# VectorE order, early loads of partial sums, and two row blocks per chunk in a fused convolution and token-mixing kernel

## The chip, the cores and the metric

The kernel runs on one core of one Trainium2 chip. The metric is device time in microseconds (us) of one execution, given as the median of several. Shorter is better. Each execution comes with the TensorE clock that was granted to the core.

The names of the engines are those of the profile: PE is TensorE (matmuls), PEld its weight loads, DVE is VectorE, ACT is ScalarE, POOL is GpSimd and SP is SyncE. An L with a number is a line of the kernel in question, so the same operation has other line numbers in other kernels.

## The reference

The inputs are x of 8 x 4224 x 192 (batch, tokens, channels), seven convolution taps for each of 8 heads, a 192 x 192 matrix for theta, two 4224 x 4224 token-mixing matrices and a 192 x 192 channel matrix. Cut to what matters:

```python
# causal 7-tap convolution over tokens, one softmaxed filter per head
x = conv(x, softmax(weight))
theta = x @ w_theta
zr = x * np.cos(theta)
zi = x * np.sin(theta)
y = np.einsum('ts,bsd->btd', w_tok_r, zr) + np.einsum('ts,bsd->btd', w_tok_i, zi)
u = x + y
return u + np.maximum(u @ w_ch, 0.0)
```

The token mixing is nearly all of the arithmetic: for each of 33 row blocks of 128 output tokens it sums over 33 chunks of 128 input tokens, for 8 x 192 = 1536 columns.

## The kernel before

The kernel makes three passes. In each it builds 11 chunks (convolution, theta, sines, products, all kept on chip), and for each of the 33 row blocks it adds those 11 chunks' share of the mixing to a partial sum in DRAM. A row block has three pieces of 512 columns, and a piece of one pass is 22 matmuls of 512 columns, so a row block of one pass has 66. The chunks of passes 2 and 3 are built in small steps between the mixing of the pass before. Only the first pass has nothing to hide its chunks behind, so its first row block is mixed chunk by chunk, in the order in which the chunks appear. In the last pass the partial sum is loaded, the convolved x is added (the residual), the mixing is added, the channel matrix is applied and the result is stored.

One chunk is a chain over three engines (cuts are marked):

```python
def build_chunk(p, c, xws, zs):
    for hp in range(H // 4):
        pc = mmps.tile([P, 2, PC], F32, name="pc", tag="mm")
        ...                                   # 8 convolution matmuls
        for k in range(2):
            nc.scalar.activation(out=xz[...], in_=pc[...], func=AT.Copy)   # L180
        yield
    ...                                       # store of xz to DRAM (xs)
    for g in range(NG):
        xTs.append(transposed(xf[:, g * GC : (g + 1) * GC]))   # 6 transposes, VectorE copy
        yield
    for g in range(NG):
        channel_mix(th, xTs[g], wth)          # 8 matmuls of 192 columns
        nc.vector.tensor_scalar(out=ang...)   # clamp
        nc.scalar.activation(out=zr[...], func=AT.Sin, ...)
        nc.scalar.activation(out=zi[...], func=AT.Sin)
        ...                                   # zr *= x, zi *= x on VectorE
        yield
```

The first row block takes three accumulators, `ys`, and mixes each chunk into all three as it appears:

```python
def chunk_major(tb, p, wts):
    ys = [yps.tile([P, PC], F32, name="y", tag="y") for _ in range(NP)]     # NP = 3
    for c in range(PASSES[p]):
        for j in range(NP):
            next(first, 0); next(first, 0)    # two steps of the chunks being built
            mix(ys[j], wts, zs[p], c, j, PASSES[p])
```

All other row blocks go through this loop. `begin_rows` loads the sums of the next row block and adds the residual, `finish_piece` evicts a finished piece:

```python
def begin_rows(tb, p):
    pv = wk.tile([P, N], F32, name="pv", tag="pv", bufs=3)
    if p:
        nc.sync.dma_start(out=pv, in_=part[p - 1][tb, :, :])
    if p == len(PASSES) - 1:
        nc.sync.dma_start(out=xr, in_=xs[rows, :])
        for j in range(NP):                                                   # L295
            nc.vector.tensor_tensor(out=pv[:, cols], in0=pv[:, cols], in1=xr[:, cols], op=ALU.add)

def finish_piece(tb, j, y, p, pv, ub):
    ...
        nc.vector.tensor_tensor(out=pv[:, cols], in0=y, in1=pv[:, cols], op=ALU.add)   # L305
    ...
        nc.scalar.activation(out=ub[:, cols], in_=pv[:, cols], func=AT.Copy)           # L310

for j in range(NP):
    for c in range(ncs):
        mix(y, wts, zs[p], c, j, ncs)
        ...            # steps of the next pass's chunks, of the output of the block before
    finish_piece(tb, j, y, p, pv, ub)
    if j == 0 and tb + 1 < NT:
        pv_next = begin_rows(tb + 1, p)
```

The order of the instructions on TensorE is pinned: each TensorE instruction gets an order dependence on the one before it, without a semaphore. On the other engines a scheduler in the framework chooses the order.

## Time and profile before

| what | before |
|---|---|
| median of 3 runs | 1776.66 us (1775.98 to 1779.78) |
| span of the profiled run | 1780.6 us, granted clock 0.970 |
| store of the first row block, pass 1 | issued at 131.4 us |
| store of the third row block, pass 1 | issued at 166.2 us |
| from there to the last store of pass 1 | 463.0 us |
| pass 2, between its last store and that of pass 1 | 513.6 us |
| last store of pass 2 to the last eviction | 630.1 us |
| period of a row block, pass 3 | 19.04 us |

The parts of the table come from the times at which SyncE issued the stores; a period is the mean distance between the first output stores of successive row blocks. In the middle of the kernel a row block is a floor: 66 matmuls at 0.2155 us are 14.2 us, and TensorE does nothing else but build the next pass's chunks. So the two ends matter.

First, the page's busy shares, and two of its rows of 40 slices (each digit is a tenth of a slice of 44.5 us; PEclk is the granted clock in tenths):

```profile
PE 1667.8 (94%) x8910; PEld 767.8 (43%) x8910; DVE 857.3 (48%) x1471; ACT 229.3 (13%) x366; POOL 517.5 (29%) x948
PE   4889999999999999999999999898888998888898
PEclk9559999999999999999999999999999999999999
```

94% looks like a kernel with 6% to gain. The Trainium skill (Perfetto Trace Analysis, section "Identifying the Most-Contended Engine") warns that the matmuls' busy share is not a good measure of how close TensorE is to its peak, because matmuls are pipelined. The slices show one reason why that holds here: in slices 2 and 3 the clock was at half, and a slow matmul counts as busy. (The 9 of the first slice is no measurement: the page takes the clock as full until the first record, and that comes at 30.7 us.) From slice 26 on, in the last pass, it falls to 8 or 9 tenths.

The windows view of before has, for each stretch, its length, then the busy time of PE, PEld, DVE, ACT and POOL with their instruction counts, the granted clock, the DMA share and GB/s. The first stretch lies in the stage in which pass 1's chunks are built, the second in the last pass:

```profile
45.00:70.00 25.00, 21.05 (x125) 9.79 (x125) 12.75 (x22) 13.08 (x23) 10.47 (x18) 0.50 0.80 111
1600.00:1700.00 100.00, 87.97 (x488) 40.72 (x486) 50.33 (x91) 9.45 (x15) 21.54 (x40) 1.00 0.61 139
```

In the stage a chunk took 10.1 us (the first transposes of successive chunks are that far apart), with the clock at 0.50 from 37.5 to 133.1 us; matmuls of 512 columns start 0.40 to 0.43 us apart there, and 0.2155 in the middle of the kernel. The waits view of before tells what the last pass waits for (engine, line, waited for: us in total, times, longest us):

```profile
DVE pv L295 <- DMA pv<-part_84: 177.2, 33, 8.6
...
PE tp L223 <- ACT ub L310: 42.9, 29, 5.8
...
PE v L235 <- DVE uT L225: 28.4, 28, 1.0
```

VectorE waits in each of the 33 row blocks, for the partial sums; that would cost nothing if nobody needed VectorE. But TensorE waits for `ub` and `uT`, which come from behind VectorE. The timeline of VectorE (start, duration, line, operation, and in brackets the idle time before it with what ended it) shows one block:

```profile
1601.51 0.56 DVE L225 COPY uT<-tp 128x768 bf16<-128x768 bf16 x1 [2.67 <-PE tp L223]
1607.04 0.69 DVE L295 TENSOR_TENSOR pv<-pv,xr 128x512 f32<-128x512 f32 x1 [4.97 <-DMA pv<-part_84]
1607.65 0.68 DVE L305 TENSOR_TENSOR pv<-y,pv 128x512 f32<-128x512 f32 x1
```

The residual addition (L295) is for the next row block. VectorE stood idle for 4.97 us before it because the sums were not there, and the eviction of the current block's finished piece (L305) stood behind it. The chain of waits shows the loop that follows (start, us, what):

```profile
1596.69 6.03 DMA out_dram<-pv
...
1602.77 4.09 DMA pv<-part_84
...
1607.04 0.10 DVE pv L295
...
1607.65 0.03 DVE pv L305
...
1614.81 0.94 DVE pv L323 x2
...
1615.77 6.09 DMA out_dram<-pv
```

The output transfer of one block (6.03 us) frees a buffer, the sums of a later block are loaded into it (4.09 us), the residual takes them, the eviction behind it follows, and from it the next output. One round is 19.1 us, and the matmuls fit into it with room to spare.

### The profile page before, as it was taken

Reading aid. Unit: us, or ns where it says so; the run is one execution under the profiler, and the core shown is the slowest. Engines: PE = TensorE matmul, PEld = TensorE weight load, DVE = VectorE, ACT = ScalarE, POOL = GpSimd, SP = SyncE. Lnnn points to the kernel's source line nnn. Section 1 sums busy time; section 2 is a strip of 40 time slices with the busy share of each in tenths; the row PEclk is TensorE's granted clock in tenths of the full one; section 3 lists DMA queues with packets and bytes.
Section 4 is the critical chain, followed back from the end, with each engine's and each line's share of the span. In section 5 each row is a group of like instructions: output and inputs, shape, how many; then the busy total and the mean of one; then the engine's idle time right before and its main releaser. Section 6 shows DMA issues by size and latency. Waiting matters only on the chain.

```text
span 1780.6 us, 22353 instructions
## 1 busy us (share of the span) xinstructions
PE 1667.8 (94%) x8910; PEld 767.8 (43%) x8910; DVE 857.3 (48%) x1471; ACT 229.3 (13%) x366; POOL 517.5 (29%) x948
## 2 busy tenths in 40 slices
PE   4889999999999999999999999898888998888898
PEld 2334444444444444444444444344444443344344
DVE  6554444444444444444444444455445445544554
ACT  3541111111111001011111111001000000000010
POOL 6414333333333233323333322222112112211210
PEclk9559999999999999999999999999999999999999
DMA  9867666666666687777887766756556655665562
GB/s 132 114 101 130 121 117 121 128 118 112 125 121 118 127 186 163 171 163 173 177 178 170 164 157 159 173 124 149 134 139 138 146 133 129 140 146 139 126 144 70
DMA packets 232807, 248.31 MB, mean 139 GB/s; under 512 B 72192, under 2 KB 207360, under 8 KB 232704
## 3 DMA queue, kind: packets, MB, share of 16 engines
q0 software_dynamic: 167616, 91.14, 41.6%
q1 hardware_dynamic: 65088, 155.77, 24.7%
q8 instruction: 69, 1.13, 0.3%
q14 instruction: 34, 0.28, 0.0%
HBM read 247.07 MB, written 90.83 MB: 190 GB/s over the span
## 4 chain that ended last, share of the span: by engine, by line
PE 59%; DMA 18%; DVE 13%; issue 2%; DVEq 0%; ACT 0%; SPq 0%
PE y L278 54%; DMA out_dram<-pv 10%; DMA pv<-part_84 8%; DVE pv L323 3%; DVE pv L295 2%; PE pc L172 1%; PE th L235 1%; DVE pv L305 1%; PE tp L223 1%; PE th L240 1%; DVE uT L225 1%; DMA part_84<-pv 1%; PE v L235 0%; PE v L240 0%; DVEq L268 0%
## 5 line engine op out<-in xcount | busy, mean ns | idle before, releaser
L259 POOL DMA_DIRECT2D st<-in_moe_w_tok_i_dram x396 | 213.8, 549 | 1036.6 <-DVE wt_10979 L268 15.9
L259 POOL DMA_DIRECT2D st<-in_moe_w_tok_r_dram x396 | 214.6, 555 | 22.5 <-issue 4.2
L305 DVE TENSOR_TENSOR pv<-y,pv 128x512 f32<-128x512 f32 x198 | 134.8, 681 | 156.9 <-PE y L278 156.8
L225 DVE COPY uT<-tp 128x768 bf16<-128x768 bf16 x132 | 72.7, 551 | 169.8 <-PE tp L223 169.5
L295 DVE TENSOR_TENSOR pv<-pv,xr 128x512 f32<-128x512 f32 x99 | 67.0, 680 | 177.2 <-DMA pv<-part_84 177.2
L209 ACT ACTIVATE zr<-ang,half_pi 128x768 bf16<-128x768 f32 x66 | 61.6, 933 | 671.0 <-DVE ang L204 671.0
L310 ACT ACTIVATE ub<-pv 128x512 bf16<-128x512 f32 x99 | 62.4, 630 | 600.8 <-DVE pv L305 600.8
L303 DVE COPY pv<-y 128x512 f32<-128x512 f32 x99 | 67.2, 678 | 109.8 <-PE y L278 109.7
L204 DVE TENSOR_SCALAR ang<-th 128x768 f32<-128x768 f32 x66 | 62.8, 952 | 96.4 <-PE th L240 96.1
L180 ACT ACTIVATE xz<-pc 128x384 bf16<-128x384 f32 x132 | 56.1, 486 | 264.9 <-PE pc L172 142.8
L223 PE MATMUL tp<-ident,ub 128*128 128x128 bf16 x396 | 38.0, 220 | 42.9 <-ACT ub L310 42.9
L235 PEld LDWEIGHTS <-uT 128*128 128x128 bf16 x528 | 39.2, 101 | 82.3 <-DVE uT L225 41.8
L235 PE MATMUL v<-wch,uT 128*128 128x192 bf16 x264 | 44.4, 250 | 28.4 <-DVE uT L225 28.4
L323 DVE SCALAR_TENSOR_TENSOR pv<-v,pv 128x384 f32<-128x384 f32 x132 | 66.0, 539 | 7.3 <-PE v L240 7.3
L223 PE MATMUL tp<-ident,xz 128*128 128x128 bf16 x396 | 41.8, 248 | 15.0 <-DVE uT L225 7.1
L223 PEld LDWEIGHTS <-ub 128*128 128x128 bf16 x396 | 27.7, 98 | 63.3 <-ACT ub L310 47.9
L212 ACT ACTIVATE zi<-ang 128x768 bf16<-128x768 f32 x66 | 54.6, 828 | 0.0
L235 PE MATMUL th<-wth,uT 128*128 128x192 bf16 x264 | 51.0, 281 | 0.0
L214 DVE TENSOR_TENSOR zr<-xz,zr 128x768 bf16<-128x768 bf16 x66 | 36.3, 550 | 29.2 <-ACT zr L209 29.2
L223 PEld LDWEIGHTS <-xz 128*128 128x128 bf16 x396 | 31.6, 111 | 37.7 <-ACT xz L180 18.4
L240 PEld LDWEIGHTS <-uT 64*128 64x128 bf16 x528 | 25.7, 94 | 47.4 <-issue 47.4
L172 PEld LDWEIGHTS <-bands 96*64 96x64 bf16 x528 | 25.8, 127 | 43.8 <-issue 25.4
(759 smaller groups left out, 3780.6 us busy)
## 6 DMA issues: line engine op xcount, KB each, us to landing
st<-in_moe_w_tok_r_dram POOLq DMA_DIRECT2D x396, 88.0 KB, 5.4
st<-in_moe_w_tok_i_dram POOLq DMA_DIRECT2D x396, 88.0 KB, 3.6
part_83<-pv SPq DMA_DIRECT2D x33, 768.0 KB, 3.3
pv<-part_83 SPq DMA_DIRECT2D x33, 768.0 KB, 7.5
part_84<-pv SPq DMA_DIRECT2D x33, 768.0 KB, 3.3
pv<-part_84 SPq DMA_DIRECT2D x33, 768.0 KB, 4.2
out_dram<-pv SPq DMA_DIRECT2D x66, 384.0 KB, 5.0
xs<-xz SPq DMA_DIRECT2D x132, 96.0 KB, 4.5
```

The costliest lines, as they stand in the source:

```text
L204: nc.vector.tensor_scalar(out=by_bank(ang[:, :, :]), in0=banks(th), scalar1=-CLAMP, scalar2=CLAMP, op0=ALU.max, op1=ALU.min,)
L209: nc.scalar.activation(out=zr[:, cols], in_=af, func=AT.Sin, bias=half_pi[:], scale=1.0)
L223: pe(nc.tensor.transpose(tp[:, k, :], u[:, k * P : (k + 1) * P], ident))
L225: nc.vector.tensor_copy(out=uT[:], in_=tp[:])
L235: pe(nc.tensor.matmul(v[k], lhsT=tT[:, 3 * q + 2 * k, :], rhs=w[:, 2 * k, :], start=True, stop=False,))
L259: nc.gpsimd.dma_start(out=st[a * Q : (a + 1) * Q, :, 0 : ncs * Q], in_=w[tb * P : (tb + 1) * P, t0 : t0 + ncs * Q].rearrange("(bt i) s -> ...
L278: pe(nc.tensor.matmul(y, lhsT=wts[m][:, c, :, :].rearrange("p bt i -> p (bt i)"), rhs=zs[c][m][:, cols], start=(c == 0 and m == 0), stop=( ...
L295: nc.vector.tensor_tensor(out=pv[:, cols], in0=pv[:, cols], in1=xr[:, cols], op=ALU.add)
L303: nc.vector.tensor_copy(out=pv[:, cols], in_=y)
L305: nc.vector.tensor_tensor(out=pv[:, cols], in0=y, in1=pv[:, cols], op=ALU.add)
L310: nc.scalar.activation(out=ub[:, cols], in_=pv[:, cols], func=AT.Copy)
L323: nc.vector.scalar_tensor_tensor(out=pk, in0=banks(v)[:, k, :, :], scalar=0.0, in1=pk, op0=ALU.max, op1=ALU.add,)
```

## The change

The change has five parts that matter here (the diff also loads the mixing weights earlier and places their transposes). They are meant to remove the in-order stall of the last pass and to fill TensorE in the stage of the first chunks.

1. From the second row block on, VectorE's order is pinned to program order, as TensorE's was. The residual is placed one piece at a time, just before the end of a piece of the row block before.
2. The sums of row block q+2 are asked for at the start of the last piece of row block q.
3. In the first stage every chunk is mixed into five accumulators: three pieces of the first row block and two of the second. All temporary results share three banks, and the chunk's steps are interleaved with the mixing.
4. The convolution's bands are built in two halves, so that the first matmul can start earlier.
5. The 16 token rows in front of a chunk (the halo) are copied on chip from the chunk before, not loaded again.

The diff, cut to its core:

```diff
-    def pe(ins): ...
+    def in_order(engine, ins):
+        if engine in last:
+            tc.add_manual_dep(ins.ins, last[engine].ins.name, NOSYNC, reason="order")
+        last[engine] = ins
+        return ins
+    pinned = [False]
+    def dve(ins):
+        return in_order("dve", ins) if pinned[0] else ins
 ...
-    for k in range(KS):
-        nc.vector.tensor_tensor(out=bview or btmp, ...)
+    for hs in (slice(0, H // 2), slice(H // 2, H)):
+        for k in range(KS):
+            nc.vector.tensor_tensor(out=bview[:, hs] if k == 0 else btmp[:, hs], ...)
 ...
+                if before is not None:
+                    nc.sync.dma_start(out=hist, in_=before.xw[lo + Q : lo + Q + HALO, h, :, :])
 ...
-    def chunk_major(tb, p, wts): ...          # three accumulators
+        open_psum(stack, 5, 3)
+        y0 = [bank("y", "y") for _ in range(NP)]
+        y1 = [bank("y", "y") for _ in range(2)]
+        def mixes(i):
+            for ys, q, c in ((y0, 0, i - 2), (y1, 1, i - 3)):
+                for j, y in enumerate(ys):
+                    if 0 <= c < nc0:
+                        mix(y, weights[q], zs[0], c, j)
+                        yield
+        for i in range(nc0 + 3):
+            ...
+            for half in range(2):
+                if old:
+                    old.theta(half)
+                next(m, 0)
+                if ch:
+                    ch.conv(2 * half)
+                    ch.conv(2 * half + 1)
+                if old:
+                    old.times_x()
+                next(m, 0)
+            ...
+        begin_rows(1)
+        begin_rows(2)
+        for j in range(2):
+            sums[1].add(j, y1[j])
+    pinned[0] = True
 ...
-                if j == 0 and tb + 1 < NT:
-                    pv_next = begin_rows(tb + 1, p)
+                if q + 1 < len(seq) and c == ncs - 2 and sums[q + 1].final:
+                    sums[q + 1].residual(j)
+                if j == NP - 1 and c == 0:
+                    begin_rows(q + 2)
```

## The prediction

> **What bounds the kernel now.** The page gives TensorE 94% busy over 1780.6 us, but the stages differ. In the timeline the 512-column mixing matmuls start 0.2155 us apart at full clock; a row block of one pass has 66, so 14.2 us. From the first and last mixing matmul of each block:
> - Start: first matmul at 13.5 us, when VectorE has finished `bands` (waits view).
> - First row block, built chunk by chunk, until 130 us. The windows view shows TensorE 84-87% busy at granted clock 0.50 from 45 to 110 us; a chunk takes 10.1 us. The chain is serial (convolution, ScalarE copy, transpose, VectorE copy, theta), with gaps of 0.7 to 1 us. The Trainium skill (TensorE: Matmul & The Clock Gate, Part 1) says the clock is halved until TensorE has been busy for a whole window of about 3.4 us; this trace agrees in that 0.50 ends at 133 us, when mixing becomes dense.
> - Rest of passes 1 and 2: 130 to 1138 us, TensorE 100% busy. 65 blocks of 14.2 plus 22 chunks at about 3.75 make 1007 us: at its floor.
> - Last pass: 1138 to 1772 us, 19.2 us a block against about 16.7 (14.2, plus twice 0.35 of transposes and 0.9 of channel mix, from the timeline). The waits view has TensorE waiting 42.9 us for `ub` and 28.4 for `uT`. The chain of waits is a loop of one block: output transfer 6.1 us, load of the partial sums into the freed buffer 4.2, then 8.8 of VectorE work in order. The scheduler put the residual addition ahead of the eviction of the current row block, so VectorE sits 5 us (177 in all) on a load while TensorE needs it.
> - Tail: 8.7 us.
>
> **What the change does.**
> 1. Pinned VectorE order, load issued a block earlier: output, sums and `xr` land about 20 to 22 us after the start of the block in which they are freed, and the residual asks for them at about 21 (estimate from 6.1, 4.2 and 6.0 us). Small VectorE waits remain, no TensorE wait. Last pass about 553 us instead of 634.
> 2. First pass: mixing for five accumulators stands between the dependent steps. Per chunk at full clock TensorE has about 5.2 us, ScalarE 5.1, VectorE 5.3, so I expect 6 to 6.5 us a chunk after a DMA-bound start (weights of three blocks, 6 us of all queues each, compete with x). At halved clock TensorE would be busy without gaps, which should release it. The stage, now with two thirds of block 2, ends at about 103 us; before, that point is about 142.
> 3. Half-size bands first: start 2 to 3 us earlier (included).
> 4. Halo on chip: a third fewer x packets (1536 to 1024 a chunk, 56 ns, 16 queues: -1.8 us of DMA); it helps only the first stage.
>
> Sum: 103 + 487 (rest of pass 1) + 510 + 553 + 9 = 1662, less 4 for the difference between profile and timing: about 1660 us, 8 in 10 between 1638 and 1692.
>
> **What would show it.** Last pass: blocks of 16.7 us, TensorE's waits for `ub` and `uT` nearly gone. First stage: granted clock near 1.0 from about 40 us, 6 to 6.5 us a chunk. Middle unchanged at 15.4 us a block.
>
> **What would make it wrong.** The clock stays at 0.50 in the first stage (+25 to 30 us); three banks for all temporary results make the chunk loop serial again; the freed buffer still comes late and the loop of output, load, residual binds (+20 to 40); in-order halo copies on the sync queue hold up sums and stores.
>
> Chances: faster by over 2% 0.96, within 2% 0.03, slower 0.01.

## The result, and the profile after

The changed kernel took 1673.88 us in the median of 4 runs (1672.72 to 1675.82), with a right result; before took 1777.4 in the same rounds. The ratio is 0.9417, with a 95% interval from 0.9401 to 0.9434. A ratio here is the mean time of one kernel's fast runs over the mean of the other's fast runs of the same rounds, so it is not quite the ratio of the medians that I quote.

| part of the profiled span, us | before | after | difference |
|---|---|---|---|
| start to the store of the third row block of pass 1 | 166.2 | 139.6 | -26.6 |
| rest of pass 1 | 463.0 | 463.0 | 0.0 |
| pass 2 | 513.6 | 510.0 | -3.6 |
| last store of pass 2 to the last eviction | 630.1 | 550.7 | -79.4 |
| the rest (tail) | 7.7 | 7.7 | 0.0 |
| span | 1780.6 | 1671.0 | -109.6 |

So nearly three quarters of the gain came from the last pass and a quarter from the first stage. The rest of pass 1 did not move. Pass 2 lost 3.6 us; it takes 510.0 in before_edge (below) too, so the order on VectorE alone gives these. A row block of the last pass took 16.73 us instead of 19.04.

The same lines of the page after:

```profile
PE 1618.1 (97%) x8738; PEld 759.3 (45%) x8910; DVE 870.9 (52%) x1550; ACT 231.0 (14%) x366; POOL 509.7 (31%) x948
PE   4889999999999999999999999999999999999998
PEclk9999999999999999999999999999999999999999
```

TensorE's row no longer falls towards the end, and no slice has a clock of 0.5. (172 matmul records are missing from this trace: 8738 against 8910 weight loads.) The windows view after, at about the same places:

```profile
45.00:70.00 25.00, 21.99 (x173) 10.48 (x175) 16.49 (x33) 14.57 (x24) 11.70 (x21) 0.89 0.94 148
1500.00:1600.00 100.00, 99.21 (x551) 47.36 (x559) 61.82 (x108) 11.33 (x18) 25.74 (x48) 1.00 0.68 161
```

In the first stretch TensorE was hardly busier than before (21.99 us against 21.05) and did 173 matmuls where it had done 125: the clock was 0.89 against 0.50. In the last pass its busy share went from 88% to 99%.

In the waits view after, the wait for the partial sums is gone, and of TensorE's waits for `ub` and `uT` in the last pass 0.4 and 0.7 us are left. Two of the lines that are left for VectorE and TensorE:

```profile
DVE pv L364 <- PE y L331: 249.3, 154, 3.5
...
PE th L276 <- ACT xz L209: 10.5, 6, 3.1
```

VectorE waits for TensorE, as it should where TensorE is the bottleneck. The second line is new, and the experiments come back to it. The timeline of VectorE in the last pass after:

```profile
1594.35 0.68 DVE L354 TENSOR_TENSOR pv<-pv,xr 128x512 f32<-128x512 f32 x1
1595.60 0.69 DVE L364 TENSOR_TENSOR pv<-y,pv 128x512 f32<-128x512 f32 x1 [0.57 <-PE y L331]
```

The residual (L354) starts without any idle time in front of it, and the eviction (L364) waits for nothing but its matmuls. The page puts the chain that ended last, by engine, as follows, before and then after:

```profile
PE 59%; DMA 18%; DVE 13%; issue 2%; DVEq 0%; ACT 0%; SPq 0%
```

```profile
PE 93%; issue 1%; ACT 1%; DVE 1%; DMA 1%; SPq 0%; DVEq 0%; ACTq 0%
```

### The profile page after: what moved, and what is told of

It is laid out like the page before. It is cut to its first block, busy times and chain, and to the rows that moved or that the text cites. A ratio compares the mean times of both kernels' runs of the same rounds, so it can differ in the third digit from the quotient of the medians.

```text
span 1671.0 us, 22525 instructions
## 1 busy us (share of the span) xinstructions
PE 1618.1 (97%) x8738; PEld 759.3 (45%) x8910; DVE 870.9 (52%) x1550; ACT 231.0 (14%) x366; POOL 509.7 (31%) x948
## 3 DMA queue, kind: packets, MB, share of 16 engines
q0 software_dynamic: 152256, 85.24, 41.7%
## 4 chain that ended last, share of the span: by engine, by line
PE 93%; issue 1%; ACT 1%; DVE 1%; DMA 1%; SPq 0%; DVEq 0%; ACTq 0%
PE y L331 84%; PE tp L260 2%; PE v L276 2%; PE v L281 1%; PE th L276 1%; PE pc L202 1%; PE th L281 1%; DMA xs<-xz 1%; ACT xz L209 0%; ACT zi L245 0%; DVE ang L237 0%; DVE uT L264 0%; SPq L220 0%; DVE zi L251 0%; DVE pv L362 0%
## 5 line engine op out<-in xcount | busy, mean ns | idle before, releaser
L364 DVE TENSOR_TENSOR pv<-y,pv 128x512 f32<-128x512 f32 x198 | 136.6, 690 | 258.6 <-PE y L331 249.3
L237 DVE TENSOR_SCALAR ang<-th 128x384 f32<-128x384 f32 x132 | 67.5, 551 | 78.9 <-PE th L281 78.9
L209 ACT ACTIVATE xz<-pc 128x384 bf16<-128x384 f32 x132 | 57.7, 487 | 285.0 <-PE pc L202 169.2
L187 POOL DMA_DIRECT2D xw<-in_x_dram x132 | 76.7, 592 | 66.4 <-PE pc L202 55.3
L354 DVE TENSOR_TENSOR pv<-pv,xr 128x512 f32<-128x512 f32 x99 | 66.3, 670 | 0.0
L276 PE MATMUL th<-wth,uT 128*128 128x192 bf16 x264 | 47.2, 259 | 10.7 <-ACT xz L209 10.5
L202 PE MATMUL pc<-xw,bands 96*64 96x192 bf16 x528 | 38.5, 264 | 15.2 <-DMA xw<-in_x_dram 12.2
L202 PEld LDWEIGHTS <-bands 96*64 96x64 bf16 x528 | 22.2, 113 | 44.5 <-issue 31.4
L260 PE MATMUL tp<-ident,xz 128*128 128x128 bf16 x396 | 37.5, 233 | 2.1 <-ACT xz L209 1.8
```

Of the source, the lines that this page charges most:

```text
L187: nc.gpsimd.dma_start(out=self.xw[lo : lo + n, h, :, :], in_=x[:, t0 : t0 + n, :].rearrange("b s d -> s b d"),)
L202: pe(nc.tensor.matmul(pc[half * 2 * Q : (half + 1) * 2 * Q, hh * B * G : (hh + 1) * B * G], lhsT=bands[:, h, :, :].rearrange("p a m -> p ( ...
L237: dve(nc.vector.tensor_scalar(out=every_other(ang[:, :, :], k), in0=pair(th[k]), scalar1=-CLAMP, scalar2=CLAMP, op0=ALU.max, op1=ALU.min,))
L260: pe(nc.tensor.transpose(tp[:, k * P : (k + 1) * P], u[:, k * P : (k + 1) * P], ident))
L276: pe(nc.tensor.matmul(v[k], lhsT=tT[:, 3 * q + 2 * k, :], rhs=w[:, 2 * k, :], start=True, stop=False,))
L354: dve(nc.vector.tensor_tensor(out=self.pv[:, cols], in0=self.pv[:, cols], in1=self.xr[:, cols], op=ALU.add,))
```

## The experiments

Twelve kernels were run, and each gave a right result. The runs below went beside the kernel before. Each expectation was put before its run; where one names a theory by a letter, the text ahead of it says in words what was in question. For nopin, one_ahead, before_pin and one_block the trace that was kept is of another execution (spans of 1770.6, 1672.5, 1697.9 and 1690.3 us) than the views quoted (1767.2, 1673.9, 1696.1 and 1688.6); it shows the same waits, and figures taken from it are marked as kept.

### What gave the gain of the last pass

The prediction gave the last pass two causes in one breath: the pinned order of VectorE, and the load that is issued a block earlier. A third possibility was that neither is needed in full, and that one pair of instructions is the matter.

**nopin.** The changed kernel, with VectorE's order left to the scheduler.

```diff
-    pinned[0] = True
+    pinned[0] = False
```

> The changed kernel with VectorE's order left to the scheduler everywhere; the load two row blocks ahead and all else kept. Built, its VectorE order again has the residual addition of row block q+2 ahead of the last eviction of row block q. Theory A (the fixed order is what frees the last pass): that addition asks for its sums about 3 to 4 us before they land, TensorE waits for ub again, blocks of the last pass take 17.5 to 19.2 us instead of 16.75, time 1700 to 1755 us. Theory B (the earlier load is what frees it): blocks stay at 16.75, time 1670 to 1680.

It took 1768.29 us (1766.84 to 1771.91), a ratio of 0.9936 (0.9921 to 0.995). The gain is nearly gone, more so than theory A had it (1755 us at most); a block of the last pass takes 19.56 us in the kept trace. The waits view of this kernel has the three lines of before again:

```profile
DVE pv L354 <- DMA pv<-part: 180.9, 33, 8.4
...
PE tp L260 <- ACT ub L368: 48.9, 30, 4.6
...
PE v L276 <- DVE uT L264: 31.9, 28, 1.2
```

So the placement of the residual in the program, and the load two row blocks ahead, are worth nothing while the scheduler moves the residual up.

**one_ahead.** The changed kernel, with the sums loaded one row block ahead, as before.

```diff
         begin_rows(1)
-        begin_rows(2)
 ...
-                if j == NP - 1 and c == 0:
-                    begin_rows(q + 2)
+                if c == 0 and j == (2 if q == 1 else 0):     # ahead of the mix
+                    begin_rows(q + 1)
```

> The changed kernel with sums and xr loaded at the start of the row block before theirs, so 9 mixing steps before the first residual addition instead of 20; order still fixed. Theory A (order): VectorE waits up to 2 us a block for xr, TensorE does not; blocks of the last pass at 16.75 to 16.9, time 1672 to 1682. Theory B (lead of the load): the loop output, load, residual comes back, blocks of 18 us or more, time 1710 or more.

It took 1674.59 us (1674.24 to 1675.63), ratio 0.9407 (0.9393 to 0.9421). The changed kernel has 0.9417. The block of the last pass takes 16.73 us in both. The earlier load is worth nothing that can be measured, and the wait of VectorE for `xr` that I had expected did not come: in the kept trace the residual has no idle time before it.

**before_pin.** The other way round: the kernel before, with VectorE's order pinned in the last pass and nothing else.

```diff
+    def dve(ins):                  # the same order dependence that pe() makes
+        if dve_on[0]: ...
 ...                                # all VectorE operations of the loop in dve(...)
+        dve_on[0] = last_pass
```

> The kernel before with VectorE pinned to program order in the last pass alone, nothing else changed. Program order there has three residual additions together, right after their load is issued at the end of a block's first piece. Naive form of theory A (any fixed order will do): last pass near 16.8 us a block, time about 1695. My form (the fixed order has to be a good one): VectorE sits 5 to 6 us on that load in every block, evictions and ub come late, 18 to 19.5 us a block, time 1740 to 1785.

It took 1698.79 us (1697.57 to 1699.89), ratio 0.9543 (0.9527 to 0.9559). My expectation was wrong. I had thought that the residual, which this kernel has at the end of the first piece in program order, would still stand and wait for sums that the late load had not brought, so that pinning alone would gain little. It gains all: the block of the last pass takes 16.66 us, and the span is 84.5 us shorter than before (82.7 in the kept trace). Two views of this kernel show why. In the timeline of SyncE the load of a block's sums is issued at 1419.38:

```profile
1419.38 0.32 SPq L299 DMA_DIRECT2D pv<-part  x1
```

and in the timeline of VectorE the residual that needs it comes at 1426.24, behind the eviction (L315), and has no idle time in front of it:

```profile
1425.63 0.69 DVE L315 TENSOR_TENSOR pv<-y,pv 128x512 f32<-128x512 f32 x1 [0.30 <-PE y L288]
1426.24 1.89 DVE L305 TENSOR_TENSOR pv<-pv,xr 128x512 f32<-128x512 f32 x3
```

I had taken the load to go out at its place in the program. It goes out when the buffer is free. In the waits of SyncE's queue the load waits for the output transfer in 30 row blocks, in the kernel before (166.3 us, line L289) and in the changed one (114.9 us, line L346). This also explains one_ahead: where the load stands in the program doesn't matter while the output transfer of an earlier block releases it.

**before_edge.** The kernel before with a single order pair: each residual addition comes after the eviction that precedes it in the program. Everything else is left to the scheduler. This run and the next were after all the others.

```diff
-            nc.vector.tensor_tensor(out=pv[:, cols], in0=y, in1=pv[:, cols], op=ALU.add)
+            evicted[0] = nc.vector.tensor_tensor(out=pv[:, cols], in0=y, in1=pv[:, cols], op=ALU.add)
 ...
-                nc.vector.tensor_tensor(out=pv[:, cols], in0=pv[:, cols], in1=xr[:, cols], op=ALU.add)
+                res = nc.vector.tensor_tensor(out=pv[:, cols], in0=pv[:, cols], in1=xr[:, cols], op=ALU.add)
+                if evicted[0] is not None:
+                    tc.add_manual_dep(res.ins, evicted[0].ins.name, NOSYNC, reason="order")
```

> The kernel before with one thing added: each residual addition is ordered after the eviction that precedes it in the program (an order without a semaphore), everything else on VectorE left to the scheduler. Theory A in its sharpest form (of the whole fixed order only this pair matters: the addition ahead of the last eviction of a block): blocks of the last pass at 16.7 us, TensorE's wait for ub gone, time 1695 to 1702, as before_pin. If other inversions matter as well: 1710 to 1780.

It took 1700.32 us (1698.5 to 1701.39), ratio 0.9547 (0.9518 to 0.9576). That is before_pin again, within its interval, with a block of 16.67 us. The timeline of VectorE in this kernel shows the pair the right way round, without a wait of the residual:

```profile
1511.33 0.69 DVE L308 TENSOR_TENSOR pv<-y,pv 128x512 f32<-128x512 f32 x1 [0.30 <-PE y L279]
1511.94 1.88 DVE L296 TENSOR_TENSOR pv<-pv,xr 128x512 f32<-128x512 f32 x3
```

**nopin_edge.** The same pair in nopin, in place of the pinned order of the whole engine. The edit is the one of before_edge, on top of that of nopin.

> nopin (1768 us) with the same single order. The built order has the residual addition of block q+2 now behind the last eviction of block q, but still ahead of the first one of block q+1. Theory A in its sharpest form: TensorE's wait for ub gone, blocks at 16.75 to 17.2 us, time 1674 to 1690, though VectorE still waits 2 to 3 us a block for the sums. If that VectorE wait is what counts: 1720 to 1770.

It took 1673.99 us (1673.81 to 1674.98), ratio 0.9402 (0.9379 to 0.9425), with a block of 16.73 us. It equals the changed kernel, and the wait of VectorE for the sums that I had expected is not there. So the whole gain of the last pass comes from one order pair, shown in both directions: taking the order away costs it, and the single pair brings it back in both kernels.

### What gave the gain of the first stage

The change mixes a second row block in the stage, so 44 matmuls of 512 columns leave the later part of pass 1. At 0.2155 us each that is 9.5 us of TensorE time that is moved into gaps. The stage gained 26.6. The question was whether the second row block is also what keeps the clock up.

**one_block.** The changed kernel, with the second row block taken out of the stage.

```diff
-        y1 = [bank("y", "y") for _ in range(2)]
 ...
-            for ys, q, c in ((y0, 0, i - 2), (y1, 1, i - 3)):
+            for ys, q, c in ((y0, 0, i - 2),):
 ...
-        for j in range(2):
-            sums[1].add(j, y1[j])
 ...
-        for j in range(2 if q == 1 else 0, NP):
+        for j in range(NP):
```

> The changed kernel, but the first stage feeds one row block; the 44 matmuls of block 2 (9.5 us at 0.2155) come after it. Theory C (a chunk of the first stage is paced by ScalarE's order and the three banks, so this mixing is free there): chunk period unchanged near 7.5 us, second row block 9.5 us longer, time 1681 to 1687. Theory D (the stage is paced by TensorE's work): chunks get 0.9 us shorter, time 1672 to 1677.

It took 1691.37 us (1688.21 to 1692.54), ratio 0.9498 (0.9484 to 0.9512): 17.5 us more than the changed kernel, where the matmuls' own time is 9.5. Both theories had it lower (1687 us at most). The third row block was stored at 159.0 us in the kept trace instead of 139.6; before it was 166.2. So of the 26.6 us of the stage some 19 need the second row block, and the other 7 came from the remaining parts of the restructured stage, which no run takes apart.

**busywork.** The changed kernel with the second row block's two accumulators mixed in the stage and then thrown away; they are mixed again in their normal place. It does more work than one_block and none of it is of use.

```diff
-        for j in range(2):
-            sums[1].add(j, y1[j])
 ...
-        for j in range(2 if q == 1 else 0, NP):
+        for j in range(NP):
```

> The changed kernel does all of its mixing in the first stage as it is, but throws away the two accumulators of block 2 and computes that block in full afterwards: 44 matmuls of useless work more than one_block, which took 1691 us, and the right result. Theory F (that mixing keeps TensorE busy enough for the clock to be granted; without it the clock stayed at 0.50 until 74 us): first row block stored at about 113 to 116 us as in the changed kernel and not at 122, time 1681 to 1686, faster than one_block in spite of more work. Otherwise (useless work costs its time): 1691 to 1701.

It took 1682.33 us (1682.17 to 1683.44), ratio 0.9432 (0.9418 to 0.9446). Useless matmuls made it 9.0 us faster than one_block by the medians, and 8.3 by the spans (1680.3 against 1688.6); the two ran on different chips, with the kernel before on both. Against the changed kernel it loses 8.5 us, which is about the 9.5 of mixing two pieces twice. The windows from 50 to 74 us show what it bought. They are those of before, one_block, busywork and the changed kernel, in this order:

```profile
50.00:74.00 24.00, 21.14 (x121) 9.57 (x121) 11.41 (x18) 9.48 (x16) 10.36 (x18) 0.50 0.96 139
```

```profile
50.00:74.00 24.00, 21.46 (x118) 8.58 (x117) 13.57 (x27) 10.48 (x19) 6.74 (x12) 0.50 0.71 122
```

```profile
50.00:74.00 24.00, 20.59 (x167) 10.31 (x172) 15.37 (x32) 14.67 (x24) 8.66 (x16) 0.93 0.86 145
```

```profile
50.00:74.00 24.00, 20.54 (x177) 9.91 (x180) 16.33 (x34) 14.79 (x25) 9.06 (x17) 0.99 0.92 155
```

The two kernels with three accumulators in the stage have a clock of 0.50 here and some 120 matmuls, the two with five have over 0.9 and some 170. The starts of the matmuls bear the records out: two matmuls of 512 columns that follow each other in the mixing start 0.40 us apart in the first two kernels and 0.226 (the median) in the others. Before stays at 0.50 from 37.5 to 133.1 us, one_block in its kept trace from 42.5 to 76.6 and in three shorter stretches later; the changed kernel from 43.7 to 50.5 and from 101.7 to 105.1.

An estimate from the trace of before seemed to fit. In the window from 45 to 70 us TensorE was idle for 16% of the time (21.05 busy of 25 us), so for about 1.6 us of a chunk of 10.1 us; two more accumulators are four more matmuls of 512 columns a chunk, which at half clock start 0.40 to 0.43 us apart in that trace, so about 1.7 us. With five accumulators there would be nothing left to idle at half clock. The Trainium skill (TensorE: Matmul & The Clock Gate, Part 1, "The HAM clock gate") says that the halved clock is the default and that a window of about 3.4 us of sustained work releases it. The length of the short stretches at 0.50 agrees with that: 3.4 us (44.5 to 47.9 in act_late, below) or twice that (43.7 to 50.5 in the changed kernel).

But the trace of before speaks against gaps as the whole reason. The two lines below are from TensorE's timeline there, each with the idle time before it in brackets. Between them TensorE worked for 7.72 us (39.88 to 47.60) without idle time, at half clock throughout:

```profile
39.88 0.80 PE L223 MATMUL tp<-ident,xz 128*128 128x128 bf16 x6 [0.65 <-DVE uT L225]
...
48.28 0.29 PE L223 MATMUL tp<-ident,xz 128*128 128x128 bf16 x1 [0.68 <-ACT xz L180]
```

The trace has eight such stretches of 7.72 us, one in each of eight chunks, and none released the clock. The first holds 6 transposes, 16 matmuls of theta, 16 of the convolution and only 6 of the mixing. And one_block, in the window shown, was busy for 21.46 of 24 us at half clock, more than the changed kernel at full clock (20.54). So the kind of the matmuls in the window may count as well; by what rule is not shown. What one_block and busywork do show is that the mixing of the second row block keeps the clock up, useful or not.

### Where the prediction's stage was too fast

The prediction had the stage end at 103 us, at 6 to 6.5 us a chunk. It ended at about 114. The first transposes of successive chunks came 10.2, 12.3 and 11.6 us apart up to 48.2 us, and after that 6.5 to 8.5. The rivals were: the order in which ScalarE takes sines and copies; the three shared banks of the temporary results; the transfers, of x and halo or of the second block's weights.

The timeline of ScalarE in the changed kernel shows one slow chunk and then part of a quick one:

```profile
59.69 0.94 ACT L242 ACTIVATE zr<-ang,half_pi 128x768 bf16<-128x768 f32 x1 [1.91 <-DVE ang L237]
60.53 0.83 ACT L245 ACTIVATE zi<-ang 128x768 bf16<-128x768 f32 x1
61.27 0.85 ACT L209 ACTIVATE xz<-pc 128x384 bf16<-128x384 f32 x2
...
67.43 0.89 ACT L209 ACTIVATE xz<-pc 128x384 bf16<-128x384 f32 x2 [1.46 <-PE pc L202]
68.22 0.93 ACT L242 ACTIVATE zr<-ang,half_pi 128x768 bf16<-128x768 f32 x1
```

At 59.69 the two sines go ahead of the copies of the convolution's results (L209), which are finished and hold two of the three banks; at 67.43 the copies go first. In the first case TensorE waits for a bank, as its timeline in the changed kernel shows:

```profile
61.78 0.24 PE L276 MATMUL th<-wth,uT 128*128 128x192 bf16 x1 [1.56 <-ACT xz L209]
```

**act_late.** The changed kernel, with ScalarE's order pinned in the stage and the sines placed behind the copies.

```diff
+    def act(ins):
+        return ins if pinned[0] else in_order("act", ins)
 ...
-            nc.scalar.activation(out=self.zr[:, cols], in_=af, func=AT.Sin, ...)
-            nc.scalar.activation(out=self.zi[:, cols], in_=af, func=AT.Sin)
-            self.late.append(cols)
+            self.af = (ang[:, :, :].rearrange("p b d -> p (b d)"), cols)
+            if pinned[0]:
+                self.sines()                  # both sines, in act(...)
 ...                                           # the copy of pc in act(...) too
                 if old:
+                    old.sines()
                     old.times_x()
```

> The changed kernel, but ScalarE's order in the first stage is pinned too: in each half of a chunk the two convolution copies come before the two sines. Theory C (in 6 of 11 chunks the scheduler put sines ahead of those copies, so the bank that the next theta needs came free 1.6 to 3 us late): TensorE's wait for xz at theta, 10.5 us, nearly gone, chunks at 6.5 to 6.8 us instead of 6.5 to 8.5, time 1660 to 1668 us. Theory E (the stage is paced by its transfers, DMA share 0.9 to 1.1 there): 1672 to 1677.

It took 1662.07 us (1661.92 to 1663.17), ratio 0.9319 (0.9304 to 0.9335). This is the best kernel. Its span is 10.9 us below that of the changed kernel, and its third row block was stored 10.8 us earlier (128.8 against 139.6), so all of it is the stage. The wait of TensorE for `xz` at theta is gone, chunks take 6.5 to 7.2 us from the fourth on, and after 37.7 us the clock was at half only from 44.5 to 47.9. The window from 50 to 74 us:

```profile
50.00:74.00 24.00, 21.56 (x188) 10.39 (x191) 16.89 (x35) 18.12 (x30) 10.92 (x19) 1.00 1.00 160
```

**mm4.** The changed kernel with four banks for temporary results and four accumulators (one of the second row block).

```diff
-        open_psum(stack, 5, 3)
+        open_psum(stack, 4, 4)
-        y1 = [bank("y", "y") for _ in range(2)]
+        y1 = [bank("y", "y") for _ in range(1)]
 ...                                  # the second block's other two pieces in their normal place
```

> The changed kernel with four banks for temporary results in the first stage and four accumulators instead of three and five; ScalarE's order is the scheduler's. With four banks theta's second half takes a bank that VectorE freed and no longer one of ScalarE's. Theory C: TensorE's wait for xz at theta gone, chunks near 6.8 us, gain 8 to 10 us, but one piece of block 2 (22 matmuls, 4.7 us) comes later: time 1666 to 1673. Theory E: 1676 to 1681. If the clock falls as in one_block (fewer mixing matmuls): up to 1685.

It took 1672.19 us (1669.5 to 1674.41), ratio 0.9373 (0.9358 to 0.9389), and its span is 1.5 us above the changed kernel's. The wait at theta is gone here too, which agrees with a bank being what theta waited for. But the convolution now waits 4.9 us for ScalarE, the clock was at half for some 20 us (45.8 to 52.7, 69.7 to 76.6, 107.3 to 114.1), and half of the moved matmuls are not moved. The run lies within what was expected of it and settles little by itself, as three things changed at once.

**halo_hbm.** The changed kernel with the halo loaded from DRAM, as before.

```diff
-                if before is not None:
+                if False:
```

> The changed kernel with the halo rows loaded from HBM for every chunk, as before the change. Theory E (transfers pace the first stage): half as many x packets again, 2 us of all queues a chunk, stage 10 to 20 us longer, time 1684 to 1695. Theory C (ScalarE order paces it): stage within 3 us, time 1670 to 1678.

It took 1668.77 us (1668.59 to 1669.8), ratio 0.9356 (0.9342 to 0.937), 4.5 us less by the spans than the changed kernel, though it loads half as much x again in the stage. That is a little below the range of theory C too, and the wrong direction for the theory that transfers pace the stage. It was not a clean test, however: the scheduler had also put ScalarE's work into a better order here, and TensorE's wait at theta was 6.2 us instead of 10.5. So the next run repeats it with that order pinned.

**act_halo.** act_late with the halo loaded from DRAM.

> act_late (ScalarE's order pinned in the first stage, 1662 us) with the halo rows loaded from HBM for every chunk. halo_hbm was 5 us faster than the changed kernel, but there the scheduler also happened to give ScalarE a better order (TensorE's wait for xz at theta 6 us instead of 10.5), so the halo's own worth is open. If that order was all of the 5 us and the copies on chip are worth nothing: 1660 to 1664. If the copies cost time: under 1660. If they save time, as I had predicted for the first stage (half as many x packets again, 2 us a chunk): 1666 to 1680.

It took 1665.36 us (1664.03 to 1665.9), ratio 0.9358 (0.9345 to 0.9371); its span is 1662.9 us against 1660.1 of act_late. That lies between the ranges that I had set. The two ran on different chips, on which the kernel before had medians of 1779.47 and 1783.94, so the ratios differ by more (0.0039, some 7 us). I go by the traces: the rest of pass 1 and pass 2 take the same time in both within 0.1 us, and the third row block is stored at 131.4 against 128.8. The copy on chip is then worth about 3 us, measured across two chips, and what halo_hbm seemed to gain most likely came with its ScalarE order.

**late_second.** act_late with the second row block's mixing, and its weights, one chunk later, in case the early transfers of three blocks' weights slow the first chunks.

```diff
-            for ys, q, c in ((y0, 0, i - 2), (y1, 1, i - 3)):
+            for ys, q, c in ((y0, 0, i - 2), (y1, 1, i - 4)):
-        for i in range(nc0 + 3):
+        for i in range(nc0 + 4):
 ...                                  # loads of block 1's and 2's weights one step later
```

> act_late with the second row block one chunk further behind, and its weights loaded one chunk later. Theory G (the first 45 us are paced by transfers and by the weights of block 2 arriving late: TensorE waits 2.5 us for wt at 42 us and chunks take 11 us): wait for wt gone, time 1655 to 1660. Otherwise (the early chunks are paced by the halved clock, or the work only moves to the end): 1660 to 1666.

It took 1665.22 us (1664.42 to 1665.7), ratio 0.9358 (0.9345 to 0.9371), span 1663.4: no gain over act_late. The first chunks came no sooner (the fourth chunk's transposes came at 42.8 us against 44.9 in act_late, but the fifth's at 53.1 against 52.1), and TensorE still waits 4.2 us for the mixing weights. This theory falls. What paces the first 45 us stays open.

## Why the prediction was right or wrong

The time was predicted as 1660 us, between 1638 and 1692, and faster by over 2% with a chance of 0.96. It was 1673.88: inside the range, 14 us above its middle. The prediction's own sum, with its boundaries, against the profile after:

| term, us | predicted | measured |
|---|---|---|
| first stage with two thirds of block 2 | 103 | about 114 |
| rest of pass 1 | 487 | 488.6 |
| pass 2 | 510 | 510.0 |
| last pass and tail | 553 + 9 | 558.4 |
| span | 1662 | 1671.0 |
| timing less span | -4 | +2.9 |

- **Last pass: the size was right, the stated cause half wrong.** Predicted were blocks of 16.7 us and no wait for `ub` and `uT`; the blocks took 16.73, and the waits are nearly gone (0.4 and 0.7 us). The step "Pinned VectorE order, load issued a block earlier" named two causes, and the size could not tell them apart, as TensorE's own work sets the block once the stall is gone (99.21 of 100 us busy). The load is worth nothing (one_ahead, 0.9407 against 0.9417), and of the pinned order it takes one pair (before_edge and nopin_edge). "Small VectorE waits remain" did not come true: VectorE's residual waits nowhere for the sums. The reading of the loop before was right in where it pointed: the residual stood ahead of an eviction that TensorE needed. It was wrong in one thought, that the load had to come earlier. Once the residual moves behind the eviction it comes late enough for the load as it is.
- **First stage: right that the mixing releases the clock, not shown why, and the term was too small.** "At halved clock TensorE would be busy without gaps, which should release it" was right in its outcome, as one_block against busywork shows. As a reason it falls short: before was busy without gaps for 7.72 us at a time and stayed at half clock. "Granted clock near 1.0 from about 40 us" came 10 us late: it was 0.50 from 43.7 to 50.5, and again for 3.4 us at 101.7. The failed step is "so I expect 6 to 6.5 us a chunk". I had added up the engines' work per chunk (5.2, 5.1 and 5.3 us) and taken it that three shared banks would let the engines run beside each other. The chunks took 6.5 to 8.5 from 48.2 us on. The prediction listed this among the things that might go wrong ("three banks for all temporary results make the chunk loop serial again") but gave it no time. With ScalarE's order fixed, 10.9 us of the stage come back (act_late), which is as much as the term was off.
- **Halo: about half of its size, and not what mattered.** Predicted were 1.8 us less DMA time a chunk. From the page's shares of the queues (41.6% and 24.7% of 1780.6 us before, 41.7% and 27.0% of 1671.0 after), the two queues that carry the data took 1181 us of all engines' time before and 1148 after, so 33 us over 33 chunks, or 1.0 a chunk. In time it was worth about 3 us by the spans (act_halo). The Trainium skill (DMA: Bandwidth & Descriptors, "Issuing engines are not separate DMA queues") says that all transfers run on the same 16 DMA engines whoever starts them, so that halo copies from another issuer still take their share; the second queue's rise from 24.7% to 27.0% agrees.
- **Half bands: about half.** The first matmul came at 12.2 us instead of 13.54, so 1.3 us earlier, where 2 to 3 were predicted.
- **Middle: right.** Pass 2 was predicted at 510 and the rest of pass 1 at 487; every kept trace with the residual behind the eviction has 510.0 within 0.1 us for pass 2, and every trace 463.0 for pass 1 after its third row block.
- **Timing against profile: wrong sign.** I had carried the 4 us by which the profiled span of before lay above its median over to the new kernel. But the profiled execution of before was itself one of the longer ones: it was timed at 1782.79 us, 6 above the median of the others, and its span of 1780.6 lies 2.2 below its own time. For the changed kernel the two are 1672.72 and 1671.0, so 1.7 apart. A timed run is some 2 us longer than its span in both, and the rest was a draw. This makes 6.9 us of the miss (the sum itself gave 1658, which I had rounded to 1660).

## What to carry to other kernels

Where an engine that works in order waits long for a transfer, ask first what stands behind the waiting instruction: here one order pair between a prefetched addition and an eviction was worth 80 us, and neither an earlier load nor a pinned order of the whole engine was needed. Mixing work that is moved into a serial stage can pay twice on TensorE, once for itself and once for the clock, and a run with useless work tells the two apart. Where several engines share a few rotating banks, the order of the engine that frees the banks belongs in the estimate, as its busy time alone does not show it.

## What the Trainium skill lacked or had wrong

- TensorE: Matmul & The Clock Gate, Part 1 ("The HAM clock gate") gives one whole idle window, about 3.4 us, as the condition for falling back to half clock. The changed kernel fell back at 101.7 us, shortly after a wait of 1.56 us (98.3 to 99.9), and at 43.7 us in the midst of another wait of 1.56 us, with one of 0.95 just before it. Much shorter gaps than a whole window are enough here. (The same part has, under "A second HAM failure mode: psum-queue depth-cycling", short idle times that make the clock change back and forth, but gives no length for them.) The length of one wait is not the rule either: two other waits of 1.56 us in this trace, which ended at 61.78 and 91.70 us, were followed by no fall.
- The same part warns that the trace's clock events can be unreliable ("HAM trace caveats"). This agrees and gives an example: in the profiled run of before_edge the mean granted clock is 0.999 and the first stage is shown at 1.00, but its first record comes at 134.2 us, and until then its mixing matmuls of 512 columns start 0.40 us apart, as in before at 0.50. Likewise, on one chip the executions of before have mean clocks of 0.968 to 0.998 with times within 0.3%. The cadence of equal matmuls decides, not the clock field.
- The same part has one window of about 3.4 us of sustained work release the clock, and does not say what counts as work. In the kernel before, TensorE worked for 7.72 us without idle time in each of eight chunks and stayed at half clock. By the windows view from 50 to 74 us, one_block was busy for 89% (21.46 of 24 us) at half clock and the changed kernel for 86% (20.54 of 24 us) at full clock. A busy share of the profile alone therefore doesn't tell which of the two states follows.
- The same page, Part 4 ("PE-mode transpose"), says that transposes do not count as busy for the clock in the same way. That may bear on the first stage, which has 12 transposes in each chunk, but no run here shows it either way.
- The same page, section "Wait — 56ns, not 53.3ns?", gives 215.7 ns between matmuls of 512 columns at full clock; the trace has 0.2155 us, so this figure agrees and needs no change.
- No page that I read says that the order chosen on one engine by the scheduler decides such a case, or that a load's place in the program may not matter: the load of the sums waited for the output transfer of an earlier block in 30 of 33 row blocks (166.3 us before, 114.9 after).
